# Top-k attention and a hard-swish feed-forward on one core: weight conversion by an integer add, left-over tiles interleaved, and a new division of PSUM

## The chip, the cores and the metric

The kernel runs on one NeuronCore of a Trainium2 chip. The core has a matrix engine (TensorE, "PE" in the profile, with its weight loads as "PEld"), three engines for elementwise work (VectorE "DVE", ScalarE "ACT", GpSimd "POOL"), and SyncE ("SP"), which here issues all DMA transfers. Each engine works through its own queue in order; semaphores make one wait for another. SBUF is the working memory. PSUM, eight banks of 512 fp32 per partition, is where PE writes; GpSimd does not read it here. The metric is the device time of one execution in microseconds (us): 1950.03 us, the median of three runs (1946.53 to 1950.18).

## What is computed

```python
# q, k, v: (8 batches, 8 heads, 576 rows, 64) fp32
scores = q @ k.T / sqrt(64)
kth    = np.partition(scores, -32, axis=-1)[..., -32:-31]   # 32nd largest of each row
scores = np.where(scores >= kth, scores, -1e9)
attn   = softmax(scores)
attn_out = attn @ v
x = attn_out.transpose(0, 2, 1, 3).reshape(4608, 512)
# w_in: (512, 2048) float64, w_out: (2048, 512) float64
h = x @ w_in
g = h * np.clip(h + 3, 0, 6) / 6
out = g @ w_out                                             # (4608, 512) fp32
```

The two weight matrices come as float64 and are made fp32 on the core.

## The kernel before

**Units.** Two heads make a pair (`Pair`, four pairs per batch, 32 in all). A pair's 576 query rows are cut into four tiles of 128 rows (`J = 4`) and a left-over tile of 64 (`R`). One tile of one pair is a unit (`Unit`). A full unit has two rows of work on every partition, one per head (`nt = 2`); a left-over unit puts the two heads on the two halves of the partitions and has one (`nt = 1`). There are 128 full and 32 left-over units. In a batch the units run tile by tile over the four pairs: sixteen full ones and then four left-over ones in even batches, the left-over ones first in odd batches. So eight left-over units stand together at every second change of batch.

**What a unit does.** `scores` (L205 to L229): PE multiplies `qT` with `kT` (512 columns) and with the pair's remaining 64 keys, which lie in a block-diagonal tile `kr` for full units (L221); ACT copies the result to SBUF. `top` (L237), four rounds on DVE: MAX8 finds the eight largest of a row of 576, MATCH_REPLACE8 strikes them out; after four rounds the 32nd largest is known. `mask` (L249) on POOL: a compare with it per row (L254), an add of the result to the scores (L259), and the negated maximum (`shift`, L262). `exp` (L264): two ACT activations with a running sum, and a small POOL add on the sum (`den`, L272). `weights` (L274): a DVE reciprocal, and two ACT activations that scale the row. `transpose` (L282): nine PE transposes into a PSUM tile, and one ACT copy out to `eT`. `values` (L293, L398): PE multiplies with v, for two units into one PSUM bank `pv`, and ACT copies that to `xT` (full) or `xr` (left-over).

**Feed-forward.** When four pairs of a tile have their values, a feed-forward over 128 tokens is due (`todo`). It is cut into eight pieces: four `h` pieces (16 matmuls each, ACT's Relu with bias 3 to `g`, and then a `gate` on DVE, L330, that reads `h` again) and four `acc` pieces of four matmuls. Left-over tiles of two batches make one feed-forward. There are 36.

**The loop** (L449 to L495) writes out the order of every queue by hand. Iteration n issues: scores of unit n+1; `weights` of unit n-2; the first round of `top` of unit n; the waiting gate; a feed-forward piece; round 2; the transposes of unit n-2; round 3; the gate; a second piece in full units; a pair's transposes (`Pair.transpose`), if due; `values` if n-2 is odd; round 4; a third piece if n%4==3; `exp` of unit n-1; `mask` of unit n.

**Weights.** `convert` (L103) takes a chunk of 128 x 512 doubles (32 chunks), one DMA to `st`. ACT makes the absolute value of the high words read as fp32 (L115), POOL clamps it (L116); ACT makes the sign, doubles it, and turns the low words into a fraction `f`, both into the PSUM tile `tr` (L120 to L123). Then, after a `yield`, that is one `convert_step` later: on DVE a shift that drops sign bits (L127), an xor with the sign (L128), an and that leaves the exponent (L129), a multiply of it with `f` (L130), and on POOL an fp32 add (L131). Three steps stand in an iteration, and three ahead of the loop.

**PSUM.** `ps_sc` one tile of three banks (scores), `ps_tr` one tile of three banks, `tr`, for the transposes of pairs and units and for the conversion (`wide`, L99), `ps_w` two single banks for `h`, `acc` and `pv`.

Of the kernel before, what the change touches and what calls it, by code (L numbers as in the profile page):

```python
# [26 lines left out]
def kernel(  # L27
# [34 lines left out]
    gpool = pool("g", 4)  # L62
    stpool = pool("st", 2)
    cvpool = pool("cv", 2)
    opool = pool("o", 1)
    ps_sc = pool("ps_sc", 1, space=PSUM)
    ps_tr = pool("ps_tr", 1, space=PSUM)
    ps_w = pool("ps_w", 2, space=PSUM)
# [9 lines left out]
    half = const([P, 1], "half")  # L78
    nc.vector.memset(half[:], 0.5)
    w_in = const([P, NHP, FF], "w_in")  # L80
    w_out = const([P, NFC, DM], "w_out")


# [3 lines left out]
    for i in range(2 * NHP):  # L87
        vm = const([P, 2, J, D], f"vm{i}")
        vr = const([P, 2, D], f"vr{i}")
        kr = const([P, 2, R], f"kr{i}")  # L90
        nc.gpsimd.memset(vr[:], 0.0)
        nc.gpsimd.memset(kr[:], 0.0)
        ring.append((vm, vr, kr))
# [4 lines left out]

    def wide():  # L99

        return ps_tr.tile([P, 3 * 512], F32, tag="tr", name="tr")

    def convert(dst, src):  # L103
# [4 lines left out]
        st = stpool.tile([P, 2 * WC], U32, tag="st", name="st")  # L108
# [3 lines left out]
        cv = cvpool.tile([P, 2, WC], F32, tag="cv", name="cv")  # L112
        a, s = cv[:, 0, :], cv[:, 1, :]
        au, su = a.bitcast(U32), s.bitcast(U32)
        nc.scalar.activation(a, hi.bitcast(F32), AF.Abs)  # L115
        nc.gpsimd.tensor_scalar(a, a, HI_MOST, HI_LEAST, ALU.min, ALU.max)  # L116
        ps = wide()
        sign, f = ps[:, 0:WC], ps[:, 512 : 512 + WC]

        nc.scalar.activation(sign, hi.bitcast(I32), AF.Sign, bias=half[:])  # L120
        nc.scalar.mul(sign, sign, 2.0)

        nc.scalar.activation(f, lo, AF.Copy, scale=2.0**-52)  # L123
# [3 lines left out]
        nc.vector.tensor_scalar(au, au, 4, 1, ALU.logical_shift_left, ALU.logical_shift_right)  # L127
        nc.vector.tensor_tensor(au, au, sign.bitcast(U32), ALU.bitwise_xor)  # L128
        nc.vector.tensor_scalar(su, au, 0xFF800000, None, ALU.bitwise_and)  # L129
        nc.vector.tensor_tensor(s, s, f, ALU.mult)  # L130
        nc.gpsimd.tensor_tensor(dst, a, s, ALU.add)  # L131
# [13 lines left out]
    class Pair:  # L145


        def __init__(self, b, hp):
            self.b, self.hp = b, hp
            self.vm, self.vr, self.kr = ring[(b * NHP + hp) % len(ring)]  # L150

        def load(self):
            h0 = 2 * self.hp
            for name, src in (("kin", k), ("qin", q)):
                t = ldpool.tile([P, J + 1, 2, D], F32, tag=name, name=name)
                setattr(self, name, t)
                for hh in range(2):
                    nc.sync.dma_start(
                        t[:, 0:J, hh, :],
# [3 lines left out]
                    t[0:R, J, :, :], src[self.b, h0 : h0 + 2, JP:S, :].rearrange("h s d -> s h d")  # L163
                )
            for hh in range(2):
# [8 lines left out]
        def transpose(self):  # L174
            kT = self.kT = kqpool.tile([P, JP], F32, tag="kT", name="kT")
            qT = self.qT = kqpool.tile([P, S], F32, tag="qT", name="qT")
            ps = wide()
# [5 lines left out]
            for i, src in enumerate((self.kin, self.qin)):  # L183
                rows = src[0:R, J, :, :].rearrange("p h d -> p (h d)")
                c0 = 2 * JP + i * R
                nc.tensor.transpose(ps[:, c0 : c0 + R], rows, ident[0:R, 0:R])
            nc.scalar.copy(kT[:], ps[:, 0:JP])
            for hh in range(2):
                d = slice(hh * D, (hh + 1) * D)
                nc.scalar.copy(self.kr[d, hh, :], ps[d, 2 * JP : 2 * JP + R])  # L190
            nc.scalar.copy(qT[:, 0:JP], ps[:, JP : 2 * JP])
            nc.scalar.copy(qT[:, JP:S], ps[:, 2 * JP + R : 2 * JP + 2 * R])

    class Unit:

# [337 lines left out]
```

## Time and profile before

| | |
|---|---|
| runs shown | 1950.03, 1950.18, 1946.53 us |
| the profiled execution, its own time | 1948.64 us |
| its span, first to last instruction | 1946.8 us |
| mean granted TensorE clock | 0.942 of full speed |
| PE busy | 1669.4 us, 86% |
| DVE busy | 1589.9 us, 82% |
| POOL busy | 1156.9 us, 59% |
| ACT busy | 1025.2 us, 53% |
| DMA | 56.5 MB, mean 29 GB/s |

"Busy" is the time in which at least one instruction of the engine runs. The names behind a line number are the program's tiles, output before input; `x288` is the number of instructions. `<-` in the table of waits names what ended an idle time: "POOL den L272 <- ACT sc L267" is POOL waiting, at line 272, for ACT's instruction of line 267. A group's duration times its count can exceed the engine's busy time, since instructions of one engine overlap at their ends. PE's matmuls are given with modelled ends. fp32 matmuls show as two instructions each, transposes as one.

### The profile page before, as it was taken

The page shows a single profiled execution, that of the slowest core. Times are in us where ns is not written, and L with a number is a line of the kernel's source. Part 1 is how long each engine was busy: PE and PEld are TensorE (multiplying, and loading weights), DVE is VectorE, ACT ScalarE, POOL GpSimd, SP SyncE. Part 2 cuts the span into 40 slices and gives each one's busy share as a digit, 9 for nine tenths or more (in the row PEclk, how much of TensorE's full clock was granted, in tenths as well). Part 3 has the DMA queues.
Part 4 walks back from the last instruction along what each step waited for, and adds up shares of the span by engine and source line. Part 5 has one row for each costly group of instructions (what it writes and reads, how often), then busy time and mean ns, then how long its engine had stood idle before and what let it go on. Part 6 is the DMA issues. An engine that isn't in the chain of part 4 may idle for free.

```text
span 1946.8 us, 30583 instructions
## 1 busy us (share of the span) xinstructions
PE 1669.4 (86%) x11648; PEld 1197.8 (62%) x11648; DVE 1589.9 (82%) x3314; ACT 1025.2 (53%) x1861; POOL 1156.9 (59%) x886
## 2 busy tenths in 40 slices
PE   2123559989999999989999999989999999989999
PEld 1022437656776677656676766657767666766666
DVE  2767679889899999789998999789998898788880
ACT  3555545545555555545555555555555555545552
POOL 1545456656666666566666666566666666656661
PEclk9556779999999999999999999999999999989999
DMA  4312220010001000011001000011001000000000
GB/s 127 105 54 84 65 61 10 19 42 19 19 19 31 25 25 6 25 43 25 7 19 30 25 24 7 25 43 25 7 19 31 24 25 6 7 7 6 7 6 12
DMA packets 101139, 56.51 MB, mean 29 GB/s; under 512 B 84096, under 2 KB 92288, under 8 KB 100992
## 3 DMA queue, kind: packets, MB, share of 16 engines
q1 hardware_dynamic: 100992, 54.55, 10.3%
q8 instruction: 92, 1.51, 0.3%
q14 instruction: 55, 0.45, 0.1%
HBM read 45.09 MB, written 9.44 MB: 28 GB/s over the span
## 4 chain that ended last, share of the span: by engine, by line
PE 36%; DVE 26%; POOL 20%; issue 14%; ACT 4%; SPq 1%; DMA 0%; POOLq 0%; DVEq 0%; ACTq 0%
PE acc L337 14%; DVE m L240 11%; POOL wk L254 10%; DVE wk L244 10%; PE h L318 8%; POOL sc L259 7%; PE pv L301 5%; PE tr L289 4%; PE ps L223 2%; DVE g L330 2%; PE ps L214 1%; ACT sc L267 1%; DVE cv L128 1%; DVE cv L130 1%; POOL den L272 1%
## 5 line engine op out<-in xcount | busy, mean ns | idle before, releaser
L254 POOL TENSOR_SCALAR wk<-sc,m 128x576 f32<-128x576 f32 x288 | 636.1, 2216 | 34.6 <-DVE m L240 17.4
L240 DVE MAX8 m<-wk 128x8 f32<-128x576 f32 x864 | 616.0, 751 | 2.7
L337 PE MATMUL acc<-w_out,g 128*128 128x512 f32 x1152 | 529.2, 603 | 0.0
L318 PEld LDWEIGHTS h<-xT,w_in 128*128 128x128 f32 x4096 | 469.2, 193 | 55.0 <-DVE g L330 32.8
L318 PE MATMUL h<-xT,w_in 128*128 128x128 f32 x4096 | 489.5, 278 | 10.3 <-DVE g L330 10.3
L244 DVE MATCH_REPLACE8 wk<-m,wk 128x576 f32<-128x576 f32 x576 | 424.6, 745 | 0.0
L259 POOL TENSOR_TENSOR sc<-sc,wk 128x1152 f32<-128x1152 f32 (+1 forms) x160 | 383.0, 2394 | 13.4
L337 PEld LDWEIGHTS acc<-w_out,g 128*128 128x128 f32 x1152 | 208.3, 190 | 261.2 <-issue 259.3
L272 POOL TENSOR_SCALAR den<-den 128x2 f32<-128x2 f32 (+1 forms) x160 | 35.3, 221 | 559.0 <-ACT sc L267 559.0
L289 PE MATMUL tr<-ident,sc 128*128 128x128 f32 x1344 | 184.4, 284 | 151.4 <-DVE cv L130 129.2
L289 PEld LDWEIGHTS tr<-ident,sc 128*128 128x128 f32 x1344 | 162.2, 147 | 203.1 <-issue 172.3
L291 ACT COPY eT<-tr 128x1152 f32<-128x1152 f32 (+1 forms) x160 | 168.8, 1055 | 175.4 <-PE tr L289 174.9
L276 DVE RECIPROCAL den<-den 128x2 f32<-128x2 f32 (+1 forms) x160 | 25.7, 161 | 253.0 <-POOL den L272 252.7
L326 ACT ACTIVATE g<-h,three 128x512 f32<-128x512 f32 x144 | 99.0, 688 | 253.1 <-PE h L318 253.1
L267 ACT ACTIVATE sc<-sc,shift 128x576 f32<-128x576 f32 x288 | 220.7, 769 | 11.6 <-POOL shift L262 11.6
L278 ACT ACTIVATE sc<-sc,den 128x576 f32<-128x576 f32 x288 | 210.4, 778 | 22.0 <-DVE den L276 21.6
L244 DVE MATCH_REPLACE8 wk<-m,sc 128x576 f32<-128x576 f32 x288 | 212.1, 744 | 0.0
L301 PE MATMUL pv<-eT,vm 128*64 128x128 f32 (+1 forms) x2560 | 172.9, 282 | 43.7 <-DVE g L330 43.1
L240 DVE MAX8 m<-sc 128x8 f32<-128x576 f32 x288 | 203.2, 743 | 0.0
L301 PEld LDWEIGHTS pv<-eT,vm 128*64 128x64 f32 x2560 | 141.7, 148 | 65.1 <-DVE g L330 47.6
L223 PE MATMUL ps<-kT,qT 64*128 64x512 f32 x512 | 150.5, 666 | 0.0
L226 ACT COPY sc<-ps 128x1024 f32<-128x1024 f32 x128 | 130.1, 1016 | 0.0
(56 smaller groups left out, 1175.3 us busy)
## 6 DMA issues: line engine op xcount, KB each, us to landing
kin<-in_k_dram SPq DMA_DIRECT2D x64, 128.0 KB, 3.0
qin<-in_q_dram SPq DMA_DIRECT2D x64, 128.0 KB, 2.8
vm<-in_v_dram SPq DMA_DIRECT2D x64, 128.0 KB, 2.3
st<-in_moe_w_in_dram SPq DMA_DIRECT2D x16, 512.0 KB, 3.9
st<-in_moe_w_out_dram SPq DMA_DIRECT2D x16, 512.0 KB, 3.5
out_dram<-o SPq DMA_DIRECT2D x32, 256.0 KB, 2.3
kin<-in_k_dram SPq DMA_DIRECT2D x32, 32.0 KB, 2.6
qin<-in_q_dram SPq DMA_DIRECT2D x32, 32.0 KB, 2.5
```

The costliest lines, as they stand in the source:

```text
L223: nc.tensor.matmul(ps[:, hh * 512 : hh * 512 + JP], pr.qT[d, qs], pr.kT[d, :])
L240: nc.vector.max(self.m[:, t, 8 * r : 8 * r + 8], self.cur[t])
L244: nc.vector.match_replace(wk, self.m[:, t, 8 * r : 8 * r + 8], self.cur[t], LOWEST)
L254: nc.gpsimd.tensor_scalar(self.wk[:, t, :], self.row[t], self.m[:, t, TOP_K - 1 : TOP_K], DROP, ALU.is_lt, ALU.mult,)
L259: nc.gpsimd.tensor_tensor(both, both, self.wk[:, 0:nt, :].rearrange("p t s -> p (t s)"), ALU.add)
L267: nc.scalar.activation(self.row[t], self.row[t], AF.Exp, bias=self.shift[:, t : t + 1], scale=scale, accum_out=self.den[:, t : t + 1],)
L278: nc.scalar.activation(self.row[t], self.row[t], AF.Copy, scale=self.den[:, t : t + 1])
L289: nc.tensor.transpose(ps[:, i * P : (i + 1) * P], self.sc[:, c0 : c0 + P], ident[:])
L291: nc.scalar.copy(eT[:, 0:n, :].rearrange("p c q -> p (c q)"), ps[:, 0 : n * P])
L301: nc.tensor.matmul(dst[hh * D : (hh + 1) * D, :], pr.vm[:, hh, c, :] if c < J else pr.vr[:, hh, :], rhs, start=(c == 0), stop=(c == J),)
L318: nc.tensor.matmul(h[:, (f - f0) * P : (f - f0 + 1) * P], w_in[:, i, f * P : (f + 1) * P], xT[:, i, :], start=(i == 0), stop=(i == NHP - 1),)
L337: nc.tensor.matmul(acc[:], gs[f // 4][:, (f % 4) * P : (f % 4 + 1) * P], w_out[:, f, :], start=(f == 0), stop=(f == NFC - 1),)
```

## The change

The diff does the following.

- **Conversion.** The sign path on ACT is dropped. ACT makes `a` (absolute value of the high words) and `f` (low words, scaled, plus 2); POOL clamps `a`. Then DVE shifts `a` left by 3 and builds `y` in one instruction from the sign bit of the high words and the bits of `f`; POOL adds `a` and `y` as int32 into the weight tile. `a` and `y` lie in the pool of `g` tiles, `f` in a `ps_w` bank, `st` in the pool of the `kT`/`qT` tiles. Two chunks are in flight instead of one, and four steps stand in an iteration instead of three.
- **PSUM.** One tile of four banks, `big`, holds in turn a pair's transposes, a unit's scores and a unit's transposes. `ps_w` has four banks. `gpool` has eight buffers.
- **Pairs.** The left-over rows of q and k lie in one tile, so that a pair has nine transposes and two copies. `kr` is gone; a full unit's scores are four matmuls, two of 512 columns and two of 64, into four banks. The loads of v have their own function; ahead of the loop they stand behind all loads of q and k.
- **Order.** After every four full units of a batch stands one left-over unit (ahead of them in odd batches). In the first eight iterations, `exp`, `weights`, `transpose` and `values` of unit n-1 stand inside iteration n. Later ones keep the distance of before. Feed-forward pieces run as soon as any are due; a left-over iteration issues one piece, a full one two, and one more if n%4==3 and n > 16. `piece` runs the waiting gate itself. `values` runs for one left-over unit alone, and for two full ones with the second first. The next batch's pairs are loaded at iterations 6, 9, 12, 15 of a batch and transposed two later.

```diff
-    ps_sc = pool("ps_sc", 1, space=PSUM)
-    ps_tr = pool("ps_tr", 1, space=PSUM)
-    ps_w = pool("ps_w", 2, space=PSUM)
+    ps_big = pool("ps_big", 1, space=PSUM)
+    ps_w = pool("ps_w", 4, space=PSUM)
...
+    def big():
+        return ps_big.tile([P, 4 * 512], F32, tag="big", name="big")
...
     def convert(dst, src):
-        st = stpool.tile([P, 2 * WC], U32, tag="st", name="st")
+        st = kqpool.tile([P, 2 * WC], U32, tag="kq", name="st")
...
-        ps = wide()
-        sign, f = ps[:, 0:WC], ps[:, 512 : 512 + WC]
-        nc.scalar.activation(sign, hi.bitcast(I32), AF.Sign, bias=half[:])
-        nc.scalar.mul(sign, sign, 2.0)
-        nc.scalar.activation(f, lo, AF.Copy, scale=2.0**-52)
+        a = gpool.tile([P, WC], F32, tag="g", name="a")
+        y = gpool.tile([P, WC], F32, tag="g", name="y")
+        f = ps_w.tile([P, WC], F32, tag="w", name="f")
+        nc.scalar.activation(a[:], hi.bitcast(F32), AF.Abs)
+        nc.gpsimd.tensor_scalar(a[:], a[:], HI_MOST, HI_LEAST, ALU.min, ALU.max)
+        nc.scalar.activation(f[:], lo, AF.Copy, bias=2.0, scale=2.0**-51)
         yield
-        nc.vector.tensor_scalar(au, au, 4, 1, ALU.logical_shift_left, ALU.logical_shift_right)
-        nc.vector.tensor_tensor(au, au, sign.bitcast(U32), ALU.bitwise_xor)
-        nc.vector.tensor_scalar(su, au, 0xFF800000, None, ALU.bitwise_and)
-        nc.vector.tensor_tensor(s, s, f, ALU.mult)
-        nc.gpsimd.tensor_tensor(dst, a, s, ALU.add)
+        nc.vector.tensor_scalar(au, au, 3, None, ALU.logical_shift_left)
+        nc.vector.scalar_tensor_tensor(
+            out=yu, in0=hi, scalar=0x80000000, in1=f[:].bitcast(U32),
+            op0=ALU.bitwise_and, op1=ALU.bitwise_or,
+        )
+        nc.gpsimd.tensor_tensor(
+            dst.bitcast(I32), a[:].bitcast(I32), y[:].bitcast(I32), ALU.add
+        )
...
         def scores(self):
-                kr = pr.kr[:].rearrange("p h r -> p (h r)")
-                nc.tensor.matmul(ps[:, 1024 : 1024 + 2 * R], pr.qT[:, qs], kr)
-                for hh, d in enumerate((h0, h1)):
-                    nc.tensor.matmul(ps[:, hh * 512 : hh * 512 + JP], pr.qT[d, qs], pr.kT[d, :])
+            for i, (s0, s1) in enumerate(((0, JP), (JP, S))):
+                for hh, d in enumerate(heads):
+                    nc.tensor.matmul(banks[:, 2 * i + hh, 0 : s1 - s0], pr.qT[d, qs], pr.kT[d, s0:s1])
...
-        tiles = list(range(J))
-        tiles = tiles + [J] if b % 2 == 0 else [J] + tiles
-        for qt in tiles:
-            units += [Unit(pairs[b, hp], qt) for hp in range(NHP)]
+        for qt in range(J):
+            full = [Unit(pairs[b, hp], qt) for hp in range(NHP)]
+            rest = [Unit(pairs[b, qt], J)]
+            units += full + rest if b % 2 == 0 else rest + full
...
     def convert_step():
-        for c in converting:
-            next(c, None)
-        converting.clear()
+        if converting and (len(converting) > 1 or not chunks):
+            next(converting.pop(0), None)
...
-        for i, u in enumerate((u0, u1)):
-            u.values(pv[:, i * w : (i + 1) * w])
+        for i, v in reversed(list(enumerate(group))):
+            v.values(pv[:, i * w : (i + 1) * w])
```

The loop after the change:

```python
    for n in range(NU + 2):
        early = n < EARLY                      # EARLY = 8
        u = units[n] if n < NU else None
        pieces = 2
        if u and u.rest:
            pieces = 1
        if n % 4 == 3 and n > 2 * EARLY:
            pieces += 1
        d = n - (1 if early else 2)
        d = d if 0 <= d < NU and n != EARLY else None
        if n + 1 < NU:
            units[n + 1].scores()
        if n < 2:
            pairs[0, n + 2].transpose()
        if d is not None and not early:
            units[d].weights()
        if u:
            u.begin()
            u.top(0)
        p = pair_at(n, 6)
        if p:
            p.load()
            p.load_values()
        convert_step()
        piece()
        if u:
            u.top(1)
        if d is not None:
            if early:
                units[d].exp()
            else:
                units[d].transpose()
        convert_step()
        if u:
            u.top(2)
        convert_step()
        if d is not None and early:
            units[d].weights()
            units[d].transpose()
        if pieces > 1:
            piece()
        p = pair_at(n, 8)
        if p:
            p.transpose()
        if d is not None:
            values(d)
        if u:
            u.top(3)
        convert_step()
        for _ in range(2, pieces):
            piece()
        if not early and 1 <= n < NU + 1:
            units[n - 1].exp()
        if u:
            u.mask()
```

## Prediction

> **What bounds the kernel now.** I read the engine table by stretches of time first, because one mean over the span hides that the run has two regimes.
>
> ```profile
> core 0: us, PE busy (x) PEld busy (x) DVE busy (x) ACT busy (x) POOL busy (x), PEclk, DMA share, GB/s
> 50.00:100.00 50.00, 6.74 (x24) 4.51 (x25) 38.06 (x76) 23.62 (x42) 29.17 (x24) 0.50 0.35 102
> 150.00:200.00 50.00, 16.41 (x103) 13.07 (x104) 35.86 (x71) 25.95 (x44) 26.37 (x24) 0.60 0.28 87
> 600.00:700.00 100.00, 97.01 (x676) 68.69 (x673) 88.00 (x187) 54.69 (x103) 63.54 (x43) 1.00 0.11 27
> 788.90:799.00 10.10, 10.10 (x41) 4.68 (x40) 5.57 (x13) 5.05 (x9) 7.58 (x7) 1.00 0.00 0
> ```
>
> Up to 300 us no engine is full: PE works 6.7 to 16 us in 50, DVE 36 to 38. From 300 us PE is busy 97% and DVE 88%. So there is a start-up bound by waits, and a steady part bound by PE with DVE close behind. The last row is one iteration whose unit is a left-over tile; it comes back below. The waits say what the start-up waits for:
>
> ```profile
> PE tr L289 <- DVE cv L130: 129.2, 8, 24.2
> PE pv L301 <- DVE g L330: 43.1, 30, 2.3
> PE tr L182 <- DVE cv L130: 16.1, 1, 16.1
> ```
>
> The attention transposes waited 129.2 us, in 8 waits, for the conversion's last DVE multiply, because both use the one `tr` tile in PSUM. The second row is the steady part's PE wait: `pv` waits until a gate frees one of two `w` banks. Third, the timeline of DVE (start of each unit's first MAX8) gives the pace. Units 1 to 8 start at 62.0, 86.4, 110.0, 140.6, 164.2, 188.0, 211.7, 241.3: some 24 to 30 us each. In the steady part four full units take 14.41+10.26+11.11+10.30 = 46.08 us, and 40 units (32 full, 8 left-over) 429.1 us (466.31 to 895.42). Eight left-over iterations together took 62.4 us of this (788.90 to 851.30): the first and the last 10.1 and 11.1, one 9.9, the others 5.8 to 6.8. Why the first took 10.1 the timeline shows:
>
> ```profile
> 788.88 4.41 POOL L254 TENSOR_SCALAR wk<-sc,m 128x576 f32<-128x576 f32 x2
> 793.37 2.63 POOL L259 TENSOR_TENSOR sc<-sc,wk 128x1152 f32<-128x1152 f32 x1
> 796.09 0.23 POOL L262 TENSOR_SCALAR shift<-m 128x2 f32<-128x2 f32 x1
> 796.94 0.78 ACT L267 ACTIVATE sc<-sc,shift 128x576 f32<-128x576 f32 x1
> 798.66 0.22 POOL L272 TENSOR_SCALAR den<-den 128x2 f32<-128x2 f32 x1 [2.25 <-ACT sc L267]
> 798.92 0.17 DVE L276 RECIPROCAL den<-den 128x2 f32<-128x2 f32 x1 [4.32 <-POOL den L272]
> ```
>
> The full unit before it is masked, exponentiated and summed while DVE has only one row to select in, 5.7 us. The chain is 7.44 us of POOL, 1.7 of ACT, and 0.4 to the reciprocal: at least 9.6 us, so DVE idles 4.3 us. Behind a left-over unit the mask is only 2.2+1.4 us, so a block of four pays once.
>
> **The change part by part. Conversion.** Per chunk ACT loses Sign 0.73 and the doubling 0.58 (L120, L121). DVE falls from 0.43+0.69+0.63+0.69 = 2.44 us (L127 to L130) to a shift (0.43, as L127) and one SCALAR_TENSOR_TENSOR with a PSUM operand (0.68, as L330): 1.11 us. POOL's clamp (0.61) stays; its add turns from fp32 (1.27, L131) to int32, which no row shows. Bounds: 0.61 (L116, one input, the same 512 elements) and 2.64 (L259, 1152 elements); I take 1.27, the same shape. The Trainium skill (GPSIMD Engine Reference, Engine selection) calls GpSimd about half as fast as VectorE for two-input elementwise work, and against that sets the exact integer add that only it has; its 4497 ns for 2048 elements would make an estimate of 1.1 us. No path of mine below changes by it.
>
> The conversion's PSUM moves to the `w` banks, so the transposes no longer queue behind it. **Prologue:** the v loads move behind all k and q loads. Pair 0's six loads are issued by 4.8 us as now and land 3.0 us later; transposes 2.25 (16.12 to 18.35 now), copies 1.3, cold scores 2.9, copies 1.3: unit 0 starts at 16.4, not 28.4. SP then decides: pair 3's load waits for pair 1's transposes (18.7), takes 3.9, and 16 v loads of 0.48 to 0.59 stand ahead of the fourth weight chunk. That chunk is issued at 32 instead of 42.45 and lands 4.4 later; Abs, clamp, shift and combine 2.4, the last MAX8s 1.4, another chunk 1.1, with gaps: unit 1 starts at 41.4, not 62.0.
>
> **Units 1 to 7.** Four chunks per unit instead of three; exp, weights and transposes of unit n-1 now stand inside unit n. The loop runs over POOL's queue: mask ends; exp 1.95; two chunks on ACT 2.6; weights 1.5; transposes 1.3; `eT` copy 1.2; Abs and clamp of the fourth chunk 1.5 with gaps, which stand ahead of the next mask 7.4. That is 17.5 us, 20.4 where `pv` and its copy lie between, 3.5 less for a left-over unit's mask. The first needs 14.9 as nothing is behind it yet. Walking through: 41.4, 56, 74, 94, 111, 128, 147, 168 for unit 8, which now starts at 241.3. With an int add of 2.64 POOL adds 5.5 us a unit, 38 in all; at 0.61 it gives back some 5.
>
> **Steady part.** For each iteration the next unit starts after the longest of three paths. (i) DVE: three rounds of 2.77 plus 1.41 = 9.7 us for a full unit, 5.7 for a left-over one (its single row hides nothing), plus 0.62 per gate. (ii) The mask chain, 9.6 us, which bites where a left-over unit follows a full one. (iii) PE's return: reciprocal and weights 1.9, transposes 1.07, second piece 3.67 (`acc` 3.54), a pair's transposes 1.1, `pv` of two units 2.4, copy to next reciprocal 2.44: 11.5 with a piece and `pv`, plus what a third piece left PE behind. On the kernel before, these rules give 46.5 for the four units measured at 46.08, so I scale by 0.992.
>
> Now the 40 iterations of two batches after the change. Left-over units are no longer in blocks: seven of eight follow a full unit, so they cost 9.6 each (one 8.2, one 10.4), 76 us against 62.4: +14. For the 32 full ones I deal out the pieces as the loop does (two, one in a left-over unit, a third at n%4==3). The queue runs dry in four iterations and is deep in others. 14 are DVE's at 9.7 to 11.0 (147 us), 18 are PE's return at 11.2 to 15.9 (221 us): 365 us after scaling, against 366.7 now. What four `w` banks give back (1.67 us of PE wait per four units now) is lost to the uneven pieces. Inside these: the scores' remainder is 0.1 us cheaper per unit (L221's 0.31 against L216's 0.28 for four, overlapping), a pair needs nine transposes for ten and 0.5 us less of ACT; and `pv` takes the fresh `eT` first, so without a second piece it waits 1.2 us for the copy, which the other order hid. **The shared four-bank tile:** scores must wait for the last `eT` copy (1.12 and 0.25 of handing over). A second piece or `pv` hides it in most iterations; where a left-over unit has one piece, PE waits 1.4 us, mostly under path (ii). Net 4 us per 40. Off the path: a left-over unit's `pv` has its own copy, 16 more of 0.27 us on an ACT that is 53% busy; the next batch's loads are issued two units, some 21 us, ahead of their transposes and land in 3, with only an output's store ahead of them on SP (uncovered, each would add its 3 us). Period: 441 us, not 429.1.
>
> **Clock.** From 855.55 to 862.01 PE had no piece; the granted clock in 861.0 to 870.7 was 0.82 and six transposes took 1.54 us instead of 0.82. Four dry iterations per 40 make more of this: 16 of them at 0.7 us are some 10 us, which I add.
>
> The Trainium skill (TensorE: Matmul & The Clock Gate, HAM oscillation) halves the clock after idle gaps over about 3.4 us, which speaks against this change; an estimate from its figures (half of a window of 3.4 us lost after each of 16 gaps) would be 27 us.
>
> **Tail.** After the last unit PE has 18 pieces left, now 12, since the last left-over feed-forward falls due just then: 6 x 3.6 = 22 us on top of the 48 (1898.8 to 1946.8).
>
> **Sum.** 168 (start of unit 8) + 124 (units 8 to 19) + 3 x 441 + 209 (last 20) + 70 + 10 = 1904 us of span. The profiled run was 1948.64 for a span of 1946.8, and the median shown, 1950.03, lies 1.4 above that: 1907, say 1906.
>
> **Rivals.**
> (A) The interleaving feeds PE as well as it feeds DVE, and path (ii) is hidden: the period stays at 429 or falls. For: PE's own work in 40 iterations is nine feed-forwards of 28.8, 32 units of 3.7, eight left-over ones of 2.6 and eight pairs of 1.2 us, 408 of the 429. Against: the 10.10 us row, which PE filled with deferred `acc` work that the new order mostly lacks. Then 1906 - 3.8 x 12 = 1860 us.
> (B) The shared tile decides, slower. `exp` stands ahead of the scores' copies in ACT's queue; if these copies are late, the transposes find the tile taken and `weights` late, and the return of every full iteration grows. It turns slower from 0.3 us in each of 150 iterations (44 us); with 0.5 the time is 1981. For: PE and ACT hand the tile over twice per unit. Against: a piece of 3.6 us lies between, and the copy is 1.2 to 1.3.
> (C) The conversion does not speed the start: the int add costs 2.64 or more and POOL's queue holds the mask back, unit 8 at 206 or later: 1944, and 1979 if unit 8 stays at 241.
>
> **Numbers.** Forecast 0.62 (own range 1870 to 1940), A 0.20, B 0.12, C 0.06. 0.2%, some 4 us, is what this measurement tells from no change. Faster: forecast and A and a third of C, 0.84; same 0.03; slower 0.13. Range 1850 to 1960: below, A; above, half of B and the add's upper bound.
>
> **What would show it.** Unit 8 starting near 168, with no wait of transposes on a conversion; left-over iterations at 9.6 with DVE waiting on `den`; a period of 441; PE's share from 300 us on at about 92%, 95% now; some 70 us of PE alone at the end. Wrong if the period is under 430 (A), if PE's waits on ACT's copies exceed 0.3 us a unit (B), or if the int add is far from 1.27 us.

## The result, and the profile after

The changed kernel takes 1967.45 us (median of four runs, 1966.45 to 1967.93), against 1950.11 us for the kernel before on the same chip. The ratio is 1.0092, 95% interval 1.0075 to 1.011: slower by 0.9%, where 1906 us had been predicted. The profiled execution has a span of 1965.2 us, against 1946.8.

Where the time went is read first from the starts of units, that is, from each unit's first MAX8 in the timeline of DVE. "Period" is the time from unit 20 to 60, 60 to 100 and 100 to 140.

| | before | predicted | after |
|---|---|---|---|
| unit 1 starts | 62.0 us | 41.4 | 40.5 |
| unit 8 starts | 241.3 | 168 | 173.3 |
| iteration 8 (to the start of unit 9) | | 9.6 | 21.7 |
| unit 20 starts | 392.4 | 292 | 310.2 |
| 40 units, three times | 429.1, 430.8, 429.1 | 441 | 456.2, 455.8, 455.5 |
| of these: 8 left-over units | 62.4 | 76 | 77.0 |
| of these: 32 full units | 366.7 | 365 | 379.2 |
| from the start of unit 140 to the end | 265.5 | 279 | 287.4 |

By unit 20 the start had gained 82 us, where 100 had been expected. Each period of 40 units then lost 26 us where 12 had been expected, and the end another 22. The difference of 61 us between the predicted span of 1904 and the measured 1965.2 adds up from +5 (unit 8), +13 (units 8 to 19), +44.5 (three periods) and +8 (the end), less the 10 us of clock that the prediction had carried as a term of its own.

The engines by stretches of time, after the change; the stretches are the first and the third of the three periods, and the time after unit 159 has started:

```profile
core 0: us, PE busy (x) PEld busy (x) DVE busy (x) ACT busy (x) POOL busy (x), PEclk, DMA share, GB/s
310.22:766.46 456.24, 415.69 (x2968) 304.98 (x2968) 378.25 (x798) 233.83 (x414) 273.89 (x201) 0.95 0.08 22
...
1222.20:1677.70 455.50, 415.18 (x2968) 304.44 (x2968) 378.21 (x797) 233.78 (x414) 273.83 (x200) 0.95 0.08 22
...
1885.38:1965.20 79.82, 75.17 (x451) 52.39 (x451) 16.07 (x33) 18.69 (x30) 14.49 (x10) 0.99 0.04 11
```

In a steady period PE now works 415.7 of 456.2 us, 91%, and its mean granted clock is 0.95. So no engine is full: in 40 us of each period PE waits. The waits of the kernel after, in us, times and the longest:

```profile
DVE den L266 <- POOL den L262: 296.0, 98, 11.9
PE big L279 <- ACT sc L268: 136.3, 27, 12.9
...
PE pv L291 <- ACT eT L281: 25.4, 21, 1.2
PE big L213 <- ACT eT L281: 25.4, 21, 1.2
...
PE big L213 <- ACT kq L184: 15.3, 12, 4.2
...
PE big L206 <- ACT kq L184: 8.9, 7, 1.3
PE big L178 <- ACT eT L281: 8.5, 7, 1.2
```

and one row of the kernel before:

```profile
DVE den L276 <- POOL den L272: 252.7, 108, 10.8
```

The wait of the transposes for the conversion (129.2 us before) is gone, and so is that of `pv` for a gate. (One wait of the transposes, 10.0 us, is put down to the conversion's add. They start there 0.87 us after ACT begins to scale the rows, as in other early units, so it is these rows that they wait for.) In their place DVE stands 296 us at the reciprocal, waiting for the sum of a softmax; after 300 us it is 274.3, where the kernel before has 202.9. PE stands 136.3 us, waiting for the scaled rows that the reciprocal releases: five of these 27 waits, 51.1 us, lie in the first 180 us, and the other 22 take 85.1 us, some 4 us each. The rows on the shared tile (`L213`, `L178` on `eT`, `L213`, `L206` on `kq`) are short and together 58 us; ahead of the loop's steady part, in the first 45 us, a pair's transposes wait another 15.3 us for a copy of scores.

What keeps the softmax is seen in iteration 31 (start of the iteration 431.64, start of the next 448.08: 16.4 us, where DVE alone would take 9.7). The timeline there, start and duration in us:

```profile
433.05 2.15 PE L279 MATMUL big<-ident,sc 128*128 128x128 f32 x9 [4.94 <-ACT sc L268]
...
442.24 3.94 PE L308 MATMUL h<-xT,w_in 128*128 128x128 f32 x32
...
446.21 0.69 ACT L316 ACTIVATE g<-h,three 128x512 f32<-128x512 f32 x1 [3.48 <-PE h L308]
446.80 0.77 ACT L257 ACTIVATE sc<-sc,shift 128x576 f32<-128x576 f32 x1
447.74 0.23 POOL L262 TENSOR_SCALAR den<-den 128x1 f32<-128x1 f32 x1 [12.10 <-ACT sc L257]
448.00 0.16 DVE L266 RECIPROCAL den<-den 128x1 f32<-128x1 f32 x1 [6.64 <-POOL den L262]
```

The `exp` of unit 30 (L257) needs only that unit's mask, which POOL had finished at 435.6. But in ACT's queue it stands behind the Relu of the iteration's third piece (L316), and the Relu waits for PE to finish that piece at 446.2. So `exp` comes 11 us late, and POOL (12.10 us idle) and DVE (6.64) with it. The first row shows the second effect: after 4.94 us without work PE's nine transposes took 2.15 us, twice the 1.15 that they take at full clock; the granted clock in these 2.15 us was 0.50. Iterations 27, 43, 51 and 55 have the same picture, with 14.4 to 16.4 us each. In those whose third piece is the last `acc` it is the output copy (L337) that stands ahead of `exp`.

Iteration 8, in which the early units' order gives way to the steady one, shows the same thing at its worst:

```profile
185.52 5.31 PE L327 MATMUL acc<-w_out,g 128*128 128x512 f32 x12
...
190.87 0.60 ACT L337 ACTIVATE o<-acc 128x512 f32<-128x512 f32 x1 [6.41 <-PE acc L327]
...
191.85 1.01 ACT L183 COPY kq<-big 128x1024 f32<-128x1024 f32 x1 [0.38 <-PE big L180]
...
192.92 0.79 ACT L257 ACTIVATE sc<-sc,shift 128x576 f32<-128x576 f32 x1
...
194.64 0.23 POOL L262 TENSOR_SCALAR den<-den 128x2 f32<-128x2 f32 x1 [13.81 <-ACT sc L257]
194.90 0.17 DVE L266 RECIPROCAL den<-den 128x2 f32<-128x2 f32 x1 [11.91 <-POOL den L262]
```

An output copy that waits for `acc`, and the copies of a pair's transposes, which PE does after that `acc`, stand ahead of `exp`; DVE has nothing to do for 11.9 us.

Two of the conversion's groups after the change, the add and the shift, with busy time and the mean of one instruction in ns:

```profile
L120 POOL TENSOR_TENSOR w_in<-a,y 128x512 int32<-128x512 int32 x16 | 20.4, 1272 | 2.0 <-DVE y L116 1.8
...
L115 DVE TENSOR_SCALAR a<-a 128x512 uint32<-128x512 uint32 x32 | 20.4, 637 | 44.5 <-POOL a L107 44.3
```

The int32 add takes 1.27 us, as the fp32 add did. The shift's mean of 637 ns mixes two lengths, to which the last section comes back.

### The profile page after: what moved, and what is told of

It is laid out like the page before. It is cut to its first block, busy times and chain, and to the rows that moved or that the text cites. A ratio compares the mean times of both kernels' runs of the same rounds, so it can differ in the third digit from the quotient of the medians.

```text
span 1965.2 us, 30832 instructions
## 1 busy us (share of the span) xinstructions
PE 1688.6 (86%) x11872; PEld 1237.7 (63%) x11872; DVE 1551.5 (79%) x3249; ACT 973.6 (50%) x1717; POOL 1160.5 (59%) x878
## 4 chain that ended last, share of the span: by engine, by line
PE 78%; POOL 9%; ACT 8%; issue 3%; SPq 1%; DMA 1%; DVE 1%; POOLq 0%; ACTq 0%
PE h L308 26%; PE acc L327 23%; PE pv L291 10%; PE big L279 8%; PE big L213 6%; POOL wk L244 5%; POOL sc L249 3%; ACT sc L257 2%; ACT eT L281 2%; PE big L206 2%; PE big L178 2%; ACT kq L183 1%; ACT sc L214 1%; ACT sc L268 1%; DMA st<-in_moe_w_in_dram 0%
## 5 line engine op out<-in xcount | busy, mean ns | idle before, releaser
L244 POOL TENSOR_SCALAR wk<-sc,m 128x576 f32<-128x576 f32 x288 | 638.1, 2223 | 30.7 <-DVE m L230 19.8
L249 POOL TENSOR_TENSOR sc<-sc,wk 128x1152 f32<-128x1152 f32 (+1 forms) x160 | 382.3, 2389 | 13.3
L279 PE MATMUL big<-ident,sc 128*128 128x128 f32 x1344 | 201.2, 297 | 168.8 <-ACT sc L268 136.3
L279 PEld LDWEIGHTS big<-ident,sc 128*128 128x128 f32 x1344 | 169.4, 154 | 212.6 <-issue 143.1
L257 ACT ACTIVATE sc<-sc,shift 128x576 f32<-128x576 f32 x288 | 221.4, 772 | 118.3 <-POOL shift L252 118.1
L281 ACT COPY eT<-big 128x1152 f32<-128x1152 f32 (+1 forms) x160 | 169.1, 1057 | 128.9 <-PE big L279 128.9
L316 ACT ACTIVATE g<-h,three 128x512 f32<-128x512 f32 x144 | 99.2, 689 | 268.4 <-PE h L308 268.3
L213 PE MATMUL big<-kq 64*128 64x512 f32 (+1 forms) x1024 | 182.3, 478 | 40.7 <-ACT eT L281 25.4
L291 PE MATMUL pv<-eT,vm 128*64 128x128 f32 (+1 forms) x2560 | 186.6, 296 | 25.4 <-ACT eT L281 25.4
L291 PEld LDWEIGHTS pv<-eT,vm 128*64 128x64 f32 x2560 | 156.0, 156 | 60.2 <-ACT eT L281 32.7
L213 PEld LDWEIGHTS big<-kq 64*128 64x128 f32 x1024 | 95.5, 202 | 141.1 <-issue 88.5
```

Source lines behind the costliest of these rows:

```text
L213: nc.tensor.matmul(banks[:, 2 * i + hh, 0 : s1 - s0], pr.qT[d, qs], pr.kT[d, s0:s1])
L244: nc.gpsimd.tensor_scalar(self.wk[:, t, :], self.row[t], self.m[:, t, TOP_K - 1 : TOP_K], DROP, ALU.is_lt, ALU.mult,)
L249: nc.gpsimd.tensor_tensor(both, both, self.wk[:, 0:nt, :].rearrange("p t s -> p (t s)"), ALU.add)
L257: nc.scalar.activation(self.row[t], self.row[t], AF.Exp, bias=self.shift[:, t : t + 1], scale=scale, accum_out=self.den[:, t : t + 1],)
L279: nc.tensor.transpose(ps[:, i * P : (i + 1) * P], self.sc[:, c0 : c0 + P], ident[:])
L281: nc.scalar.copy(eT[:, 0:n, :].rearrange("p c q -> p (c q)"), ps[:, 0 : n * P])
```

## The experiments

Four things were left to tell apart: the interleaved order itself, the shared four-bank tile, the places of `exp` and of the values in the queues, and PE's half clock after dry gaps. All ratios are against runs of the kernel before on the same chip (medians 1949.3 to 1950.1 us). "Half clock" is the time after 300 us in which the trace's clock records grant 0.5 (they show only 1.0 and 0.5, and the last runs up to 2 us past the last instruction). Some expectations name theories by letters: Q, `exp` stands behind other work in ACT's queue; T, the shared tile makes PE and ACT take turns; L, the 9.5 us of each left-over unit are the whole loss.

| kernel | us | ratio, 95% interval | unit 20 | period | left-over + full | half clock |
|---|---|---|---|---|---|---|
| before | 1950.1 | | 392.4 | 429.1 | 62.4 + 366.7 | 43 us |
| the change | 1967.45 | 1.0092 (1.0075 to 1.011) | 310.2 | 456.2 | 77.0 + 379.2 | 188 |
| change, left-over units in blocks | 1848.16 | 0.9485 (0.9471 to 0.9499) | 311.6 | 427.7 | 68.5 + 359.2 | 27 |
| before, interleaved | 2146.62 | 1.1017 (1.0998 to 1.1035) | 400.4 | 484.5 | 75.4 + 409.1 | 207 |
| before, new arithmetic | 1901.05 | 0.976 (0.9745 to 0.9774) | 345.3 | 430.8 | | 48 |
| the same, no PSUM for it | 1873.21 | 0.9616 (0.9601 to 0.963) | 316.9 | 430.8 | | 42 |
| change, `exp` early | 1908.76 | 0.9791 (0.9777 to 0.9806) | 308.1 | 441.2 | 88.6 + 352.6 | 140 |
| change, `exp` ahead of third piece only | 1952.35 | 1.002 (1.0011 to 1.003) | 309.4 | 452.6 | 77.8 + 374.7 | 177 |
| change, values in order | 1921.67 | 0.9863 (0.9845 to 0.9882) | 302.4 | 445.4 | 74.5 + 370.9 | 139 |
| change, unread matmuls | 1931.69 | 0.9914 (0.9897 to 0.9931) | 306.5 | 448.2 | 74.9 + 373.3 | 37 |
| change, `exp` early and unread matmuls | 1888.49 | 0.9695 (0.9679 to 0.9712) | 304.1 | 435.1 | 90.0 + 345.0 | 7 |
| change, all three | 1874.25 | 0.9613 (0.9597 to 0.9629) | 300.0 | 433.7 | 89.0 + 344.7 | 16 |
| blocks, unread matmuls | 1847.81 | 0.9482 (0.9468 to 0.9496) | 310.9 | 427.7 | | 4 |
| blocks, `exp` early | 1836.96 | 0.943 (0.9416 to 0.9444) | 307.2 | 428.0 | 68.2 + 359.9 | 23 |
| blocks, `exp` early, values in order | 1806.09 | 0.9268 (0.9254 to 0.9282) | 300.4 | 421.3 | 68.1 + 353.2 | 24 |

Periods are the first of the three; the others lie within 5 us.

**Interleaving undone, and interleaving alone.** The first edit gives the changed kernel the old order of units, the second gives the kernel before the new one (its pieces, its two `w` banks and its loads kept; a left-over unit has its own `pv`).

```diff
-        for qt in range(J):
-            full = [Unit(pairs[b, hp], qt) for hp in range(NHP)]
-            rest = [Unit(pairs[b, qt], J)]
-            units += full + rest if b % 2 == 0 else rest + full
+        tiles = list(range(J))
+        tiles = tiles + [J] if b % 2 == 0 else [J] + tiles
+        for qt in tiles:
+            units += [Unit(pairs[b, hp], qt) for hp in range(NHP)]
```

> The change, with the left-over units in blocks as before. Theories Q and L: the third piece is again the first acc piece of a feed-forward, left-over chains are paid once per block; 40 units take 420 to 430 us, the tail is as before (64 us from the start of the last unit), the run 1845 to 1880 us. Theory T: 40 units stay above 440 us, the run 1900 to 1950.

Measured 1848.16 us, with a period of 427.7. This one part of the change costs 119 us, and the rest of the change gains 102 us over the kernel before. The block order uses the same shared tile, twice per unit, and its period is below the 429.1 of before: the shared tile alone does not make a kernel slow. PE's waits on its copies are 40 us there, for the 58 in the change. The windows of this kernel:

```profile
311.56:739.30 427.74, 403.63 (x3002) 296.47 (x3001) 378.71 (x799) 234.40 (x415) 273.74 (x201) 1.00 0.09 23
1786.50:1846.20 59.70, 54.37 (x336) 37.50 (x334) 14.49 (x31) 16.79 (x27) 14.52 (x10) 0.99 0.03 10
```

Beside the rows of the change, the 28.5 us of a period split in two: PE's own work is 12.1 us shorter (403.6 for 415.7, much the same matmuls at clock 1.00 for 0.95), and its idle time 16.4 us (24.1 for 40.5). The last row is the tail, 59.7 us for 79.8: twenty more.

> The kernel before, with the left-over units interleaved as in the change (its pieces and PSUM tiles kept, values of a left-over unit alone). Theories Q and L: slower than before by what the steady part lost, 40 units 445 to 460 us, the start as before, the run 2010 to 2050 us. Theory T: 40 units 425 to 440 us, the run 1940 to 1980.

Measured 2146.62 us, worse than expected: a period of 484.5, 55 us over the kernel before, where the change's own order loses 28.5. This kernel has the old, separate tiles, so interleaving costs without the shared one too. One wait that grows:

```profile
PE pv L301 <- DVE g L330: 79.3, 43, 2.8
```

It was 43.1 us before: with two `w` banks the uneven stream of pieces runs into its gates. That is 36 of 196 us. DVE's wait at the reciprocal grows more, from 252.7 to 425.2 us, and the half clock from 43 to 207. So something in the rest of the change makes interleaving less dear; whether it is the four banks, the piece rule or another part was not separated.

**The conversion.** In the kernel before, the arithmetic alone is exchanged (shift by 3, sign bit merged with the bits of `f`, int32 add), with `f` first still in the tile `tr`, then in SBUF:

```diff
-        nc.scalar.activation(sign, hi.bitcast(I32), AF.Sign, bias=half[:])
-        nc.scalar.mul(sign, sign, 2.0)
-        nc.scalar.activation(f, lo, AF.Copy, scale=2.0**-52)
+        nc.scalar.activation(f, lo, AF.Copy, bias=2.0, scale=2.0**-51)
```

> The kernel before with the new conversion arithmetic alone: f stays in the transposes' PSUM tile, one chunk in flight, three steps in an iteration, order and PSUM as before. Theory A (the arithmetic is what shortens the start: 1.3 us of DVE and 1.3 of ACT less for each of 32 chunks): unit 8 starts at 190 to 215 us instead of 241, the run 1905 to 1930. Theory R (room and order shorten it: the conversion's own PSUM bank, two chunks in flight, the early distance of one unit): unit 8 at 225 or later, the run 1930 to 1950.

> The same as e5_conversion_alone, but f lies in SBUF, so the conversion holds no PSUM tile and the transposes never queue behind it. Theory A: within 10 us of e5_conversion_alone. Theory R: 15 to 40 us faster than it, unit 8 at 180 to 205, transposes no longer wait on the conversion's DVE instructions (129 us in the kernel before).

Measured 1901.05 and 1873.21 us; unit 8 starts at 200.8 and 176.0, against 241.3 before and 173.3 in the change, and the periods stay at 429 to 431. So the shorter arithmetic brings 40.5 us of the gain at unit 8, and taking the conversion out of the transposes' tile another 25. Both theories were right in part: A has unit 8 of the first kernel, R the 28 us between the two. The second kernel's unit 8 lies 2.7 us behind the change's, so two chunks in flight, a fourth step and the early order together bring little up to there. In the first kernel the wait on the tile is smaller and still there:

```profile
PE tr L285 <- DVE cv L123: 96.4, 8, 21.0
```

**The place of `exp`.** In the changed kernel `exp` of unit n-1 is issued ahead of the second piece instead of at the end of the iteration; in a second kernel it is moved past the third piece alone; in a third, the first edit is made in the block order.

```diff
+        if not early and 1 <= n < NU + 1:
+            units[n - 1].exp()
         if pieces > 1:
             piece()
...
         for _ in range(2, pieces):
             piece()
-        if not early and 1 <= n < NU + 1:
-            units[n - 1].exp()
```

> The change, with exp of unit n-1 issued ahead of the iteration's second piece instead of at its end. Theory Q (queue: the Relu or output copy of a third piece, and the pair's copies, stand ahead of exp in ACT's queue and put PE's third piece on the loop): the iterations of 14 to 16 us in n%4==3 go, 40 units take 425 to 440 us instead of 456, unit 8 to 9 takes 10 to 12 us instead of 21.7, the run 1870 to 1910 us. Theory T (the shared four-bank tile serialises PE and ACT): 40 units stay at 450 or more, 1950 to 1970. Theory L (the 9.5 us of each left-over unit is the whole loss): 40 units stay at 450 or more too, since the left-over iterations stay.

> The change, with exp issued only ahead of the third piece. Theory Q: the part of the excess that is the third piece goes, 40 units 436 to 446 us, the run 1900 to 1935; unit 8 to 9 stays near 20 us, since no third piece is in it. Theories T and L: 1955 to 1970.

> The change with both edits that helped: left-over units in blocks, and exp issued ahead of the second piece. Theory Q: with exp off PE's path the four-unit period falls from some 46 us towards PE's own 45 and DVE's 41 to 43, 40 units 412 to 422 us, the run 1795 to 1830. If exp's place only matters where a third piece is a Relu or the last acc, which the blocks do not have: 40 units at 425 to 428, the run 1838 to 1850.

Measured 1908.76, 1952.35 and 1836.96 us. Moving two lines gives back 59 us of the change and 15 us of its periods; passing the third piece alone gives 15 us of time, 4 to 5 of a period, where 10 to 20 of a period had been expected. So the Relu or output copy of the third piece is not the whole cost. In the first period of that run the eight full iterations with a third piece fall from 110.2 to 86.5 us, but the eight full ones right after them rise from 90.2 to 107.9 (iterations 31 and 32: 12.3 and 14.4 us, for 16.4 and 10.9): `exp` no longer waits for the third piece, and the next iteration waits for PE instead. With `exp` ahead of the second piece too these sums are 80.7 and 98.5.

In the block order the early `exp` brings 11 us, most of it in iteration 8 (10.7 us for 18.5) and little in the periods (428.0, 424.5 and 425.4 for 427.7, 427.6 and 427.8). Theory Q had expected 412 to 422 there; the other case of that expectation, 425 to 428, is the one that came, with a time 1 us under its range. Iteration 31 in the changed kernel with `exp` early:

```profile
431.14 0.78 ACT L257 ACTIVATE sc<-sc,shift 128x576 f32<-128x576 f32 x1
...
432.10 0.23 POOL L262 TENSOR_SCALAR den<-den 128x1 f32<-128x1 f32 x1 [1.07 <-ACT sc L257]
...
436.67 0.14 DVE L266 RECIPROCAL den<-den 128x1 f32<-128x1 f32 x1
```

The sum of the softmax is there 4.3 us before DVE asks for it, and the reciprocal has no idle time ahead of it: iteration 31 takes 9.7 us for 16.4. Iteration 32 takes 13.3 for 10.9, so PE's third piece is paid for there in part, and the two together give 4.4 us back. PE's wait for the scaled rows falls from 136.3 to 95.9 us in all, some 50 of which lie in the first 180 us in both.

**The order of the values.** The change computes the younger of the two units of a `pv` first. Undone, in the change and in blocks with `exp` early:

```diff
-        for i, v in reversed(list(enumerate(group))):
+        for i, v in enumerate(group):
```

> Blocks and exp early as in the run of 1836.96 us, and the two units of a pv computed in order, so that the older eT is used first. If PE's return path sets the pace of the full units there: PE's 51 us of pv waiting for the eT copy nearly go and the time falls to 1820 to 1832 us, the period from 426 to about 422. Rival: the wait lies beside DVE's rows and costs nothing: 1835 to 1840 us.

> The change with the two units of a pv computed in order (the older eT first) and nothing else altered. In blocks with exp early the same edit gained 30.9 us, as much as PE's wait of pv on eT fell (50.6 to 20.4). If that wait costs its length here too: PE waits 25.4 us in 21 places in the change, nearly all full units without a second piece between, so 15 to 25 us come back: 1942 to 1953 us. If the wait lies inside longer idle time of PE (its dry gaps, its half-speed clock): 1960 to 1968 us.

Measured 1806.09 and 1921.67 us, 30.9 and 45.8 us less, both more than expected. In blocks PE's wait of `pv` on the `eT` copy falls from 50.6 us in 48 places to this:

```profile
PE pv L291 <- ACT eT L281: 20.4, 23, 0.9
```

That is 30.2 us less for 30.9 us of time, as it would be if PE's return path (reciprocal, scaled rows, transposes, `pv`) set the pace of the full units and every microsecond of the wait counted. In the change the wait of 25.4 us disappears altogether and 45.8 us come back, with the half clock down from 188 to 139 us. That a shorter gap also spares PE slow windows would explain the surplus; the two weren't separated here.

**The clock.** Where an iteration's first piece finds no feed-forward due, 16 matmuls of weight columns with the identity fill a `w` bank that nobody reads. They are put into the change, into the change with `exp` early, and into the block order as a control.

```diff
+    def filler():
+        fill = ps_w.tile([P, 512], F32, tag="w", name="fill")
+        for f in range(16):
+            c = (f % 4) * P
+            nc.tensor.matmul(fill[:, c : c + P], w_in[:, 0, f * P : (f + 1) * P], ident[:])
...
-        piece()
+        if not piece() and EARLY < n < NU:
+            filler()
```

> The change, with 16 matmuls into an unread PSUM bank wherever the first piece of an iteration finds no feed-forward due, so that PE does not idle there; nothing else. Theory H (the half-speed clock after dry gaps is part of the steady loss): the mean clock rises from 0.933 to 0.95 or more, 40 units take 445 to 452 instead of 456, the run 1935 to 1958. Theory Q (order alone): the clock may rise, but 40 units stay at 455 or rise by the 3.7 us of a filler where PE is late, the run 1963 to 1990.

> The change with exp issued ahead of the second piece, and the 16 unread matmuls in iterations whose first piece finds no feed-forward due. If the half-speed clock and exp's place are two separate losses: 1875 to 1892 us, a period of 432 to 437 instead of 441, and half-speed time after 300 us of 40 us or less instead of 140. If what is left with exp early is only the mask chain at the left-over units, the filler brings nothing: 1903 to 1915 us.

> The change with left-over units in blocks, and the same unread matmuls. Control for the filler: the block order has 27 us of half-speed clock after 300 us, so if the filler works by the clock it brings next to nothing here: 1844 to 1858 us (1848.16 without). If it works by something else, such as PE's order against ACT, it should gain here too: 1835 us or less.

Measured 1931.69, 1888.49 and 1847.81 us. Useless work makes the change 36 us faster, and the change with `exp` early 20; in the block order, which has only 27 us of half clock to lose, it changes nothing (1848.16 without). As a control this is weak, since only 4 iterations run dry there, for 20 in the change. That the filler works by the clock is seen better in PE's own work. A period holds five fillers, this row (those instructions alone, from unit 20 to 60):

```profile
306.53:754.73 448.20, 19.20 (x163) 18.25 (x162) 0.99 0.09 22
```

PE is busy 424.3 us in that period; without the fillers that is 405.1, for 415.7 in the change. Over three periods PE's other work is 33 us shorter and the periods are 25 us shorter. In the change with the filler the wait that was 136.3 us reads

```profile
PE big L279 <- ACT sc L268: 51.3, 5, 12.9
```

which are the five waits of the start: later on the fillers stand where PE had waited. One window over the three periods shows the clock at 0.99:

```profile
306.53:1653.40 1346.87, 1273.95 (x9416) 944.60 (x9416) 1138.41 (x2398) 703.12 (x1244) 824.39 (x603) 0.99 0.09 22
```

The Trainium skill (TensorE: Matmul & The Clock Gate, HAM oscillation) charges half of the throttled time as the penalty. Half of the 151 us of half clock that the filler removed would be an estimate of 75 us; 36 were measured, so here the measurement decides. The 36 us are what is left after 20 fillers of 3.8 us, some of which may delay work, and PE waits in part of that time anyway; the runs do not separate the two.

**All three in the interleaved order.** This run decides whether the interleaved order has a further cost.

> The change, interleaved, with exp ahead of the second piece, the values in order and the unread matmuls in dry iterations. If the full units' 378.8 us per 40 were these three things and nothing else, what is left above the block order is the mask chain at the left-over units (77 against 62 us per 40) and the tail: a period of 423 to 430 us, full units at 346 to 353, a time of 1840 to 1862 us. If the order of the values only filled time that the chain takes anyhow: no gain over 1888 us, 1880 to 1890.

Measured 1874.25 us: neither range held. The full units come to 344.7 us per 40, 1 us under what was expected if these three things were all of their excess, but the left-over ones to 89 instead of 77, and the period stays at 433.7, 12 to 16 us over the block order with the same `exp` and values. In time the two differ by 68 us: 43 in the three periods, 22 after the start of unit 159, 2 between. So the three things do not explain all of the 119 us; this part of the interleaved order's cost none of them removes. The eight left-over iterations take 8.7 to 14.5 us. Iteration 44, the longest (from 552.05 to 566.54), shows what happens in it:

```profile
553.76 3.70 PE L327 MATMUL acc<-w_out,g 128*128 128x512 f32 x8
...
557.39 1.30 PE L213 MATMUL big<-kq 64*128 64x512 f32 x8
...
558.62 3.84 PE L308 MATMUL h<-xT,w_in 128*128 128x128 f32 x32
558.72 0.23 POOL L252 TENSOR_SCALAR shift<-m 128x2 f32<-128x2 f32 x1
...
562.50 0.69 ACT L316 ACTIVATE g<-h,three 128x512 f32<-128x512 f32 x1 [1.19 <-PE h L308]
...
563.48 1.12 ACT L281 COPY eT<-big 128x1152 f32<-128x1152 f32 x1 [0.29 <-PE big L279]
564.49 0.78 ACT L257 ACTIVATE sc<-sc,shift 128x576 f32<-128x576 f32 x1
```

The third piece of iteration 43 (`acc`, first row) leaves PE 5.3 us into iteration 44 when it comes to the scores. The mask of the full unit 43 is done at 558.95, but its `exp` now stands behind the first piece's Relu and behind the `eT` copy, and starts at 564.49, 5.5 us late. It is the same fault in another place: this left-over iteration, with 5.7 us of work for DVE, is too short to hold the work that PE has been dealt, and whatever stands behind PE in ACT's queue is late. That the other seven are long for the same reason was not read.

## Why the prediction was wrong

- **The steady part, path (iii), is the step that failed.** It was taken as the pieces and transposes of PE plus a fixed 2.44 us to the next reciprocal, and gave 365 us for the 32 full units; they measured 379.2, which over three periods is 43 of the 61 us. The path had no place for ACT's queue: the prediction named what is queued behind `exp` (rival B), but not what `exp` is queued behind. The run with `exp` early took 26.6 us off the full units (352.6) and put 11.6 on the left-over ones, 15.0 off the period. The scaling by 0.992 on the old order could hardly show this: in blocks, in the kernel after, the same move takes only 1.7 us off a period, on the mean of three.
- **The value order inside path (iii) was named and under-weighed.** "It waits 1.2 us for the copy, which the other order hid" has the right length (25.4 us in 21 places), but it was put inside a sum that netted out. Undone alone it is worth 45.8 us.
- **The clock was sized at 10 us for the whole run.** 188 us at half clock after 300 us, against 43 before, and 36 us of time by the filler say that it is more than three times that. The prediction counted 16 dry iterations at 0.7 us for one set of transposes; the filler found 20, and in iteration 31 the transposes alone lost 1.0 us, and what followed them ran slow too. The 27 us that the prediction gave beside its own figure and set aside lay nearer.
- **Iteration 8** took 21.7 us for 9.6, by the same queue: 12 us, once.
- **The left-over chain was right:** 77.0 us for 76 per 40, 9.5 us in seven of eight, with DVE waiting on `den`. But the runs with `exp` early show that this cost moves (89 + 345) when the full units shrink, so it is not a fixed price for each left-over unit.
- **The start was right in its mechanism and nearly in size:** unit 1 at 40.5 (41.4), unit 8 at 173.3 (168), no wait of transposes on a conversion. The loop took 16.2 to 23.3 us where 17.5 to 20.4 had been worked out. The shift took 0.64 us on the mean for the 0.43 put down, of which the last section has more. Rival C falls: the add took 1.27 us.
- **The tail was right, the last 20 units were not.** The prediction counts the tail from the reciprocal that opens the iteration after unit 159's (1898.79 in the kernel before, 48 us ahead of the end). Here that reciprocal starts at 1895.84, and the tail is 69.4 us for 70. The last 20 units up to there took 218.1 us, where 209 had been put down (217.5 before).
- **Rival A falls** with a period of 456. **Rival B** had as its mark PE's waits on copies of the shared tile above 0.3 us a unit. They are 58 us over 160 units, 0.36, and the time was slower as B had it; yet B's cause does not hold: the block order keeps the shared tile, with 0.25 us a unit of such waits, and beats the kernel before by 5%, and interleaving costs with the old separate tiles too. The mark was wrongly drawn, since it does not ask whether such waits lie on the path. An interleaved kernel with the change's other parts and separate tiles was not run.
- **Where the expected gain went:** the block order with the rest of the change gains 102 us. Interleaving takes 119: 84 us in three periods (27.7 to 28.5 each), 20 after the start of unit 159 and 16 between units 140 and 159, less 1 us that it gains at the start. The fastest version found keeps the blocks, issues `exp` ahead of the second piece and computes the values in order: 1806.09 us, 0.9268 of the time before.

A row of that version, from unit 20 to 60, is the counterpart of the first fence: PE works 406.1 of 421.3 us, 96%.

```profile
300.42:721.70 421.28, 406.12 (x3001) 298.13 (x3001) 377.74 (x798) 235.42 (x414) 273.42 (x200) 0.99 0.09 24
```

## What to carry to other kernels

When units of different length are interleaved, walk each in-order queue, not only the engine's own busy time: for every instruction on the critical path ask what stands ahead of it in its queue and for whom that one waits. An instruction that needs only an early result belongs ahead of one that waits for the longest piece on PE. Then look at the next iteration too: here the time that `exp` gained by passing the third piece was mostly paid there. In this kernel a stream of pieces that ran dry cost the gap and then the slow clock after it: the interleaved order ran dry in 20 iterations after 300 us, the block order in 4.

## What the hardware showed beyond that

- 16 unread matmuls in each of 20 iterations without a feed-forward piece made the kernel 36 us faster (1967.45 to 1931.69), and four such fillers changed nothing where the clock was already up (1848.16 and 1847.81).
- DVE's shift on 128 x 512 uint32 took 427 ns in the kernel before (two shifts in one instruction) and 427 and 424 ns in the kernels with the new arithmetic alone (one shift). In the change, with the same single shift, the mean is 637 ns, but the median is 427 too: 23 of the 32 took 0.40 to 0.43 us, and seven took 1.03 to 1.49. Each of these seven ran beside GpSimd's add and ended some 0.3 us after it (one more started in an add's last 0.1 us and took 0.40), as here:

```profile
54.60 1.27 POOL L120 TENSOR_TENSOR w_in<-a,y 128x512 int32<-128x512 int32 x1
54.66 1.49 DVE L115 TENSOR_SCALAR a<-a 128x512 uint32<-128x512 uint32 x1
```

- Beside GpSimd's compare (L244, one tensor input) the shift kept its 0.41 to 0.43 us in seven of eight cases and took 0.62 in the other. In the kernel before the `and` of the same shape (L129) took 2.83 us instead of 0.43 in the two cases in which it started while GpSimd's add of two tensors (L259, 2.61 us) was running. No run moved one of these instructions alone.
- The int32 add on GpSimd took 1264 to 1272 ns in the change and the two kernels with the new arithmetic alone, the fp32 add of the same shape 1269.
